# Retention followed by a SwiGLU layer on one core: the start as one list of single-engine steps, with the first pair of group 1 earlier and float32r products in five units

## The chip, the cores and the metric

The kernel runs on one core of a Trainium2 chip. The metric is the device time of one execution in microseconds (us), lower is better. A time is given as the median of three runs; the profile is of one execution of its own.

## What is computed

Four sequences of 768 tokens with 8 heads of 64 go through a retention layer (attention with a decay per head, kept as a running state from block to block). Its output, 3072 rows of 512, is normalised by its root mean square and goes through a gated layer with 1536 hidden units:

```python
for b in range(nb):
    intra = np.einsum('bhic,bhjc->bhij', qb, kb) * Dmask[None]
    intra = np.einsum('bhij,bhjd->bhid', intra, vb)
    inter = np.einsum('bhid,bhde->bhie', qb * lam_pow[None], kv_state)
    out[:, :, sl] = intra + inter
    kv_state = lam_block * kv_state + np.einsum('bhsd,bhse->bhde', kb_dec, vb)
rms = np.sqrt(np.mean(x * x, axis=-1, keepdims=True) + 1e-06)
xn = x / rms * rms_g
g = xn @ w_gate
silu = g * (1.0 / (1.0 + np.exp(-g)))
return (silu * (xn @ w_val) @ w_out).astype(np.float32)
```

## The kernel before

The rows are handled in six groups of 512 tokens. A group's retention is done in four pairs of heads (class `Pair`): `scores` (8 matmuls into `pa`, line 449), `decay_k` on ACT, `decay_a` on DVE (`a` from `pa` and the mask, L463), `decay_q` (L468), `state_sums` (`pst`, L477), `states` (L490, L492), `mix` (`po`, L504 and L512) and `keep`, which copies the output to `x` and squares it. `Norm` turns the squares into sums (`pss`, L565), a power on POOL (L576), and a spread over the partitions (`pr`, L582); then `high` (L624, L627) and `low` (L630) write x as an fp16 part `xh` and an fp16 rest `xl`.

The hidden layer is done in units of 128 hidden columns, 12 to a group (class `Hidden`). `gate` and `val` are 12 matmuls of 128x512 in fp16 each: in part 0 the high part of the weight by `xh`, in part 1 its low part by `xh`, in part 2 its high part by `xl`. `silu` is on ACT (L729), `mul` on DVE (L736), and `out` adds the unit's product with its rows of w_out into four accumulators. For `out` there are two forms: with `mul(True)` the hidden values stay float32 and each of the four matmuls is a float32 one against whole w_out rows (L659). Otherwise `high` (L746, ACT) and `low` (L753, DVE) split them into float32r parts, `split_o` (L238 on ACT, L239 on DVE) splits w_out likewise, and each tile is three float32r matmuls (L662 to L664).

Weights come as 64-bit numbers and are rebuilt on the chip (class `Weights`): `lift` on ACT (L214), `convert` on DVE (L223, L226), `square` on ACT (L382), a column-norm matmul (`pn`, L386), `scale` on DVE (L393, L397), then `high` on ACT (L404), `low` on DVE (L408), and `undo` (L414, L415). `lift_o` and `convert_o` do the same for w_out.

The order on all engines is written out by hand. Each call puts its instructions into the queues of its engines, which run them in that order. The order of the units is: group 0's units 0 to 5, all of group 1, group 0's units 6 to 11, then groups 2 to 5. `first_group` does group 0's four pairs, its norm and the first weights. `busy(n)` puts n float32 matmuls, which nobody reads, into PE's queue at the start (5 and 4) and around the norm (8 and 3). Then `first_unit`, `second_unit`, `scarce_unit` (three times) and `last_scarce_unit` do units 0 to 5 of group 0; all six use `mul(True)`. From unit 1 on each of the first four does one pair of group 1, and each converts the weights of the next unit. The units of group 1 do `split_o` for w_out's first six blocks. Loads are issued on SP, in an order that buffers decide: `load_next` takes the next one off a list.

Of the kernel before, what the change touches and what calls it, by code (L numbers as in the profile page):

```python
# [9 lines left out]
F32 = mybir.dt.float32  # L10
# [7 lines left out]
P = 128  # L18
# [5 lines left out]
def retention_swiglu_kernel(  # L24
# [67 lines left out]
    def load_gv(f):  # L92
        if f == 0:

            t = partial.bitcast(I32).rearrange("p a (b w) -> p (a b) w", w=2)
            t = t.rearrange("p (k o) w -> p k o w", k=2)
            for i in range(2):
                nc.sync.dma_start(t[:, i], w_all[f, :, i])
        else:
            t = stage.tile([P, 2, G, 2], I32, tag="in", name=f"raw_gv_{f}", bufs=4)  # L100
            nc.sync.dma_start(t, w_all[f, :, 0:2])
        raws[f] = t
# [10 lines left out]
    load_o(0)  # L113
    load_o(1)


    pending = []
    for i in range(NP):
        pending += [(load_gv, i + 1), (load_qkv, 1, i)]
# [35 lines left out]
    def powers(p):  # L155
        for h in (2 * p, 2 * p + 1):
# [4 lines left out]
        nc.vector.tensor_tensor_scan(  # L161
            pw[:, p, :], lam_p[:, p : p + 1].broadcast_to([P, P]), zeros, 1.0,
            ALU.mult, ALU.add,
        )
# [8 lines left out]
    def scales():  # L173
        gmax = const.tile([P, 1], F32, name="gmax")
# [3 lines left out]

        pmax = ps_out.tile([P, DM], F32, tag="po3", name="pmax")
        nc.tensor.matmul(pmax[:, :P], gmax.broadcast_to([P, P]), ident, start=True, stop=True)  # L180
        powers(0)
        nc.vector.tensor_reduce(gmax, pmax[:, :P], axis=mybir.AxisListType.X, op=ALU.max)
        ge = const.tile([P, 1], I32, name="ge")
        nc.vector.tensor_single_scalar(ge, gmax.bitcast(I32), 0x7F800000, op=ALU.bitwise_and)
        nc.vector.tensor_scalar_min(ge, ge, float(252 * EXP))
        sx = const.tile([P, 1], F32, name="sx")
# [49 lines left out]
    def split_o(f):  # L236
        wo[f] = t = wpool.tile([P, 2, DM], F32R, tag=f"wo{f}", name=f"wo_{f}")
        nc.scalar.copy(t[:, 0], whole_o(f))  # L238
        nc.vector.tensor_sub(t[:, 1], whole_o(f), t[:, 0].bitcast(F32))  # L239
# [103 lines left out]
    class Weights:  # L343


        def __init__(self, f, halves=False):
            self.f = f
            self.raw = raws.pop(f).rearrange("p k w o -> p (k w) o")
            if halves:

                ws = [op.tile([P, G], I32, tag="o", name=f"w_{f}_{i}") for i in range(2)]
            else:
                self.w = cvt.tile([P, 2 * G], I32, tag="w", name=f"w_{f}")
                ws = [self.w[:, i * G : (i + 1) * G] for i in range(2)]
            self.wi = ws
            self.ws = [w.bitcast(F32) for w in ws]
            self.ssq = small.tile([P, 2], F32, tag="ssq", name=f"ssq_{f}")
            self.bits = whole_o(f).bitcast(I32)

        def lift(self, i=None):  # L360
            if i is None:
# [14 lines left out]
        def convert_o(self):  # L376
            convert(self.bits, self.raw_o)
            load_o(self.f + 2)

        def square(self, i):  # L380
            junk = cvt.tile([P, G], mybir.dt.bfloat16, tag="junk", name=f"junk_{self.f}_{i}")
            nc.scalar.activation(junk, self.ws[i], AF.Square, accum_out=self.ssq[:, i : i + 1])  # L382

        def norm(self, pn, c=slice(0, 2)):
            self.pn = pn
# [20 lines left out]
        def low(self, i):  # L406
            hi, lo = ((wg, wv)[i][:, self.f, j] for j in range(2))
            nc.vector.scalar_tensor_tensor(  # L408
# [13 lines left out]
        def split(self):  # L422
            pn = ps_att.tile([P, 2, G], F32, tag="ps", name=f"pn_{self.f}")
            self.norm(pn[:, 0])
# [10 lines left out]
    class Pair:  # L435
# [3 lines left out]
        def __init__(self, m, p):  # L439
            self.m, self.p = m, p  # L440
            self.qT, self.kT, self.k, self.v = loaded.pop((m, p))
            self.odd = m == 0 and p % 2
# [11 lines left out]
        def decay_k(self):  # L454
            for j, r in enumerate(heads):
                last = mask[:, 2 * self.p + j, P - 1 : P]
# [8 lines left out]
        def decay_q(self):  # L465
            eng = nc.vector if self.m < 2 and (self.m, self.p) != (1, 0) else nc.gpsimd
# [30 lines left out]
        def mix(self):  # L497
            m, p = self.m, self.p
# [3 lines left out]
            for c in range(GC):  # L502
                for j, r in enumerate(heads):
# [3 lines left out]
                    )  # L507
            for c in range(GC):
# [8 lines left out]
        def keep(self):  # L517

            m, p = self.m, self.p
            if p == 0:  # L520
                x = xpool.tile([P, NK, G], F32, tag=f"x{SLOT_OF[m]}", name=f"x_{m}")
                if m:
                    sq = xpool.tile([P, GC, P], F32, tag="sq", name=f"sq_{m}")
                else:
                    sq = tmp.tile([P, GC, P], F32, tag="t", name=f"sq_{m}")
                rows[m] = x, [sq]
            x, sums = rows[m]
            sq = sums[0]
            s1 = sq
            if p:  # L530
                s1 = tmp.tile([P, GC, P], F32, tag="t", name=f"sq_{m}_{p}")
            if p < NP - 1:
                nc.scalar.copy(x[:, p, :].rearrange("p (c i) -> p c i", c=GC), self.po)
            nc.scalar.activation(s1, self.po, AF.Square)
            if p == NP - 1:
                nc.scalar.copy(x[:, p, :].rearrange("p (c i) -> p c i", c=GC), self.po)
            if m == 0 and p == NP - 1:
                sums.append(s1)
            elif p:
                last = m == 1 or p == NP - 1  # L540
                (nc.vector if last else nc.gpsimd).tensor_add(sq, sq, s1)
            load_next()

    class Norm:
# [11 lines left out]
        def sums(self, i=0):  # L556

            if i == 0:
                pss = ps_att.tile([P, 2, G], F32, tag="ps", name=f"pss_{self.m}")
                self.pss = pss[:, 0]  # L560
# [9 lines left out]

        def root(self):
            m = self.m
            ms = small.tile([P, GC], F32, tag="ms", name=f"ms_{m}")
            nc.vector.tensor_scalar(ms, self.pss4, 1.0 / DM, 1e-6, ALU.mult, ALU.add)
            self.y = small.tile([P, GC], F32, tag="y", name=f"y_{m}")
            nc.gpsimd.tensor_tensor(self.y, ms, power, op=ALU.pow)  # L576

        def spread(self):
            pr = ps_att.tile([P, 2, GC, P], F32, tag="ps", name=f"pr_{self.m}")[:, 0]
# [40 lines left out]
        def high(self, kk):  # L620
# [6 lines left out]
            nc.scalar.copy(self.xh[:, kk, :], xn)  # L627
# [4 lines left out]
        def parts(self):  # L632
            for kk in range(NK):
                self.high(kk)
# [64 lines left out]
    def finish(m, f, hh, hl, half):  # L699
        first = f == 0 or (m == 0 and f == HALF)  # L700
        last = f == NF - 1 or (m == 0 and f == HALF - 1)
        for t in range(GC):
            out_product(m, f, hh, hl, t, first, last, m == 0, half)

    class Hidden:


        def __init__(self, m, f):
            self.m, self.f = m, f
            self.half = m > 1  # L710
            self.x = xs[m]
# [5 lines left out]
        def gate(self, part=None, between=None):  # L717
            if not part:
                self.pg = ps_gv.tile([P, G], F32, tag="pg", name=f"pg_{self.m}_{self.f}")
            product(self.pg, *self.w[0], *self.x, part, between)  # L720

        def val(self, part=None, between=None):
            if not part:
                self.pv = ps_gv.tile([P, G], F32, tag="pv", name=f"pv_{self.m}_{self.f}")
            product(self.pv, *self.w[1], *self.x, part, between)
# [29 lines left out]
        def out(self):  # L755
            finish(self.m, self.f, self.hh, self.hl, self.half)
# [8 lines left out]
    def first_group():  # L765

        pair = [None] * NP
        busy(5)
        scales()
        busy(4)  # L770
        for p in range(NP):
            pair[p] = new = Pair(0, p)
            new.scores()
            new.decay_k()
            if p == NP - 1:
                wt = Weights(0)
                wt.lift()
            new.decay_a()
            if p < NP - 1:
                powers(p + 1)  # L780
            new.decay_q()
            if p:
                pair[p - 1].mix()
                pair[p - 1].keep()
            new.state_sums()
            new.states()
        new.mix()
        wt.convert(part=0)
        new.keep()
        nxt = Weights(1, True)  # L790
        nxt.lift(0)
        nxt.lift(1)
        norm = Norm(0)
        norm.sums(0)
        norm.sums(1)
        norm.root()
        wt.convert(part=1)
        wt.square(0)
        wt.square(1)
        busy(8)  # L800
        norm.spread()
        nxt.convert(0)
        nxt.square(0)
        pn = ps_out.tile([P, DM], F32, tag="po3", name="pn_0")
        wt.norm(pn)
        wt.scale()
        wt.high(0)
        norm.high(0)
        wt.high(1)
        norm.high(1)  # L810
        norm.high(2)
        norm.high(3)
        norm.low(2, nc.gpsimd)
        norm.low(3, nc.gpsimd)
        busy(3)
        nxt.norm(pn[:, 2:], slice(0, 1))
        wt.low(0)
        wt.low(1)
        wt.undo()
        nxt.scale(slice(0, 1))  # L820
        norm.low(0)
        norm.low(1)
        return wt, nxt

    def first_unit(h, wt_o, wt):

        h.gate(0)
        h.val(0)
        h.gate(1)
        h.val(1)  # L830
        wt.high(0)
        h.gate(2)
        h.val(2)
        wt.low(0)
        wt_o.lift_o()
        wt.convert(1)
        h.silu()
        wt.square(1)
        wt_o.convert_o()

    def second_unit(h, before, wt_o, wt, new):

        h.gate(0)
        wt_o.norm(ps_att.tile([P, 2, G], F32, tag="ps", name=f"pn_{wt_o.f}")[:, 0], slice(1, 2))
        h.gate(1)
        h.gate(2)
        wt_o.scale(slice(1, 2))
        wt_o.high(1)
        before.mul(True)
        wt_o.low(1)  # L850
# [253 lines left out]
```

## Time and profile before

| | |
|---|---|
| median of 3 runs | 685.96 us (685.9 to 686.19) |
| the profiled execution's own time | 685.8 us |
| its span, first to last instruction | 684.0 us |
| busy: PE, DVE, ACT, POOL | 673.3, 329.9, 246.2, 61.9 us |
| loaded and stored by DMA | 50.97 MB |

The span is the time between the first and the last instruction that the profiler saw; 1.8 us of the profiled execution lie around it. Busy times are sums over the whole span; PE is TensorE's matmuls, PEld its weight loads, which run beside them.

### The profile page before, as it was taken

Reading aid. Unit: us, or ns where it says so; the run is one execution under the profiler, and the core shown is the slowest. Engines: PE = TensorE matmul, PEld = TensorE weight load, DVE = VectorE, ACT = ScalarE, POOL = GpSimd, SP = SyncE. Lnnn points to the kernel's source line nnn. Section 1 sums busy time; section 2 is a strip of 40 time slices with the busy share of each in tenths; the row PEclk is TensorE's granted clock in tenths of the full one; section 3 lists DMA queues with packets and bytes.
Section 4 is the critical chain, followed back from the end, with each engine's and each line's share of the span. In section 5 each row is a group of like instructions: output and inputs, shape, how many; then the busy total and the mean of one; then the engine's idle time right before and its main releaser. Section 6 shows DMA issues by size and latency. Waiting matters only on the chain.

```text
span 684.0 us, 9838 instructions
## 1 busy us (share of the span) xinstructions
PE 673.3 (98%) x4118; PEld 359.5 (53%) x4118; DVE 329.9 (48%) x589; ACT 246.2 (36%) x434; POOL 61.9 (9%) x56
## 2 busy tenths in 40 slices
PE   8899999999999999999999999999999999999997
PEld 7645555556566555554444555444465444444443
DVE  6877677557557586644732322551332371221112
ACT  4656447545544523545222222231322231211111
POOL 0310000000002101434000111000012000000000
PEclk9999999999999999999999999999999999999999
DMA  8725652224213301223000131100100000100001
GB/s 322 294 93 171 278 197 93 92 93 154 63 62 124 124 1 40 73 75 114 10 1 1 62 123 63 62 1 1 61 2 1 0 1 1 61 1 1 0 1 61
DMA packets 14300, 50.97 MB, mean 75 GB/s; under 512 B 1712, under 2 KB 1968, under 8 KB 12848
## 3 DMA queue, kind: packets, MB, share of 16 engines
q1 hardware_dynamic: 13968, 49.69, 20.1%
q10 hardware_dynamic: 288, 0.66, 0.3%
q8 instruction: 32, 0.52, 0.3%
q14 instruction: 12, 0.10, 0.1%
HBM read 44.05 MB, written 6.29 MB: 74 GB/s over the span
## 4 chain that ended last, share of the span: by engine, by line
PE 96%; DVE 3%; POOL 0%; issue 0%; ACT 0%; DVEq 0%; POOLq 0%
PE pg L643 27%; PE pv L643 27%; PE acc L662 9%; PE acc L664 8%; PE acc L663 8%; PE pa L449 3%; PE acc L659 3%; PE po L504 3%; PE po L512 3%; PE pst L477 2%; DVE a L463 1%; PE unread L146 1%; PE pss L565 0%; DVE xn L624 0%; DVE state L492 0%; PE pr L582 0%
## 5 line engine op out<-in xcount | busy, mean ns | idle before, releaser
L643 PE MATMUL pg<-x,wg 128*128 128x512 f16 x864 | 199.9, 379 | 2.7 <-ACT x L627 1.6
L643 PE MATMUL pv<-x,wv 128*128 128x512 f16 x864 | 199.0, 379 | 0.0
L736 DVE SCALAR_TENSOR_TENSOR sg<-pv,cv,sg 128x512 f32<-128x512 f32 x48 | 36.0, 750 | 220.5 <-PE pv L643 220.5
L643 PEld LDWEIGHTS <-wg 128*128 128x128 f16 x864 | 82.6, 98 | 104.8 <-issue 9.2
L643 PEld LDWEIGHTS <-wv 128*128 128x128 f16 x864 | 84.5, 98 | 100.5 <-issue 0.4
L729 ACT ACTIVATE sg<-pg,cg 128x512 f32<-128x512 f32 x72 | 49.3, 685 | 150.6 <-PE pg L643 150.2
L664 PE MATMUL acc<-wo,hh 128*128 128x512 f16 (+1 forms) x264 | 101.2, 383 | 0.0
L663 PE MATMUL acc<-wo,hh 128*128 128x512 f16 (+1 forms) x264 | 101.1, 383 | 0.0
L746 ACT CAST hh<-sg 128x512 f16<-128x512 f32 (+1 forms) x66 | 40.8, 618 | 160.0 <-DVE sg L736 160.0
L662 PE MATMUL acc<-wo,hh 128*128 128x512 f16 x192 | 72.9, 380 | 0.0
L468 POOL TENSOR_TENSOR qkv<-qkv,pw 128x512 f32<-128x512 f32 x17 | 21.9, 1286 | 305.3 <-PE pa L449 305.3
L753 DVE TENSOR_TENSOR hh<-sg,hh 128x512 f16<-128x512 f32 x48 | 33.8, 703 | 24.6 <-ACT hh L746 24.6
L463 DVE TENSOR_TENSOR a<-pa,mask 128x1024 f32<-128x1024 f32 x24 | 29.4, 1224 | 8.0 <-PE pa L449 8.0
L662 PE MATMUL acc<-wo,hl 128*128 128x512 f32 x72 | 31.3, 435 | 0.0
L662 PEld LDWEIGHTS <-hh 128*128 128x128 f16 x192 | 18.8, 98 | 23.5 <-issue 2.4
L664 PEld LDWEIGHTS <-hh 128*128 128x128 f16 x192 | 18.8, 98 | 22.6
L663 PEld LDWEIGHTS <-hh 128*128 128x128 f16 x192 | 18.8, 98 | 20.8
L449 PE MATMUL pa<-qkv 64*128 64x128 f32 x384 | 27.9, 285 | 1.0 <-DVE a L463 1.0
L449 PEld LDWEIGHTS pa<-qkv 64*128 64x128 f32 x384 | 23.3, 187 | 10.1 <-issue 8.5
L504 PE MATMUL po<-a,qkv 128*64 128x128 f32 x384 | 25.7, 276 | 0.4 <-DVE a L463 0.4
L736 DVE SCALAR_TENSOR_TENSOR sg<-pv,cg,sg 128x512 f32<-128x512 f32 x18 | 13.5, 748 | 24.1 <-PE pv L643 24.1
L457 ACT ACTIVATE qkv<-qkv,mask 128x256 f32<-128x256 f32 x48 | 21.6, 500 | 5.3 <-DVE mask L157 3.3
(133 smaller groups left out, 629.4 us busy)
## 6 DMA issues: line engine op xcount, KB each, us to landing
qkv<-in_qkv_dram SPq DMA_DIRECT2D x47, 512.0 KB, 4.8
raw_gv<-in_weights_dram SPq DMA_DIRECT2D x11, 1024.0 KB, 7.6
raw_o<-in_weights_dram SPq DMA_DIRECT2D x12, 512.0 KB, 4.1
out_dram<-o SPq DMA_DIRECT2D x23, 256.0 KB, 2.5
partial<-in_weights_dram SPq DMA_DIRECT2D x2, 512.0 KB, 12.7
qkv<-in_qkv_dram ACTq DMA_DIRECT2D x1, 512.0 KB, 4.0
out_dram<-o SPq DMA_DIRECT2D x1, 128.0 KB, 2.1
out_dram<-o ACTq DMA_DIRECT2D x1, 128.0 KB, 2.0
```

What stands on the lines that cost most here:

```text
L449: nc.tensor.matmul(self.pa[:, j, c, :], self.kT[r, c, :], self.qT[r, c, :], start=True, stop=True,)
L463: nc.vector.tensor_mul(self.a, self.pa, decay.broadcast_to([P, 2, GC, P]))
L468: eng.tensor_mul(self.qT, self.qT, pw[:, p : p + 1, :].broadcast_to([P, GC, P]))
L504: nc.tensor.matmul(po[r, c, :], self.v[:, c, r], self.a[:, j, c, :], start=c == 0, stop=False, skip_group_check=True,)
L643: nc.tensor.matmul(ps, w[:, kk, :], x[:, kk, :], start=i == kk == 0, stop=i == 2 and kk == NK - 1,)
L662: nc.tensor.matmul(acc, hl[:, ts_], oh, start=first, stop=False)
L663: nc.tensor.matmul(acc, hh[:, ts_], ol, start=False, stop=False)
L664: nc.tensor.matmul(acc, hh[:, ts_], oh, start=False, stop=last)
L729: nc.scalar.activation(self.sg, self.pg, AF.Silu, scale=cg[:, self.f, 0:1])
L736: nc.vector.scalar_tensor_tensor(out, self.pv, factor, self.sg, ALU.mult, ALU.mult)
L746: nc.scalar.copy(self.hh, self.sg)
L753: nc.vector.tensor_sub(self.hl, self.sg, hh)
```

## The change

`first_group` and the six unit functions are replaced by one function, `ramp`, which calls single steps of pairs, norms, weights and units one after another. For that, methods are cut into parts that use one engine each (`mix` into `mix_chunks` and `mix_states`, `keep` into `keep_output`, `keep_squares` and `add_squares`, `high` of the norm into `scaled` and `high`, `split_o` into `high_o` and `low_o`, `powers` into three, `out` takes a list of tiles). What is done differently beyond the order:

- group 1's first pair (`p10`) has all its matmuls before the first gate matmul of group 0;
- units 0, 2, 3, 4 and 5 of group 0 use the float32r form of `out`, with their parts of w_out split in this stage; unit 1 stays float32;
- `out` is called tile by tile, between parts of other units' gate and val;
- the `busy` matmuls are kept in number (5, 4, 3, 8), with the first five after `pmax`;
- group 0's `decay_q` is on POOL, two of its `low` parts that were on POOL are on DVE, and the powers are all computed before the first `decay_a`;
- qkv of group 1's first pair is loaded before the weights of unit 1, and w_out's first blocks after those.

```diff
-    load_o(0)
-    load_o(1)
+    pending = [(load_qkv, 1, 0), (load_gv, 1)]
+    for i in range(1, NP):
...
-        if h.m == 1 and h.f < HALF:
+        if h.m == 1 and h.f < HALF and h.f not in wo:
             split_o(h.f)
...
+        largest()
+        pm = scales()
+        powers(0, 0)
...
+        p00.decay_k()
+        busy(5)
...
+        p00.scores()
+        busy(4)
+        p00.decay_a()
+        p00.decay_q(nc.gpsimd)
...
+        n0.sums(0)
+        n0.sums(1)
+        w0.square(0)
+        n0.mean()
+        w1.lift(0)
+        w1.lift(1)
+        p10.scores()
+        load_next()
+        p10.decay_a()
+        busy(3)
+        busy(8)
+        w1.convert(0)
+        w0.square(1)
+        w0.pn = w1.pn = ps_out.tile([P, DM], F32, tag="po3", name="pn_0")
+        w0.norm()
+        w1.convert(1)
...
+        p10.decay_q(nc.gpsimd)
+        p10.mix_states()
+        h0.gate(0)
+        h0.gate(1)
+        h0.val(0)
...
+        h0.out(3)
+        h0.out(0)
+        p10.keep_squares()
+        h2.val(1)
+        h0.out(1)
```

What this does to the queues shows at three places. PE, from the sums of group 0's squares to the first gate matmul. Before (`busy` is the tile `unread`, `pn` a column norm):

```order
L565 MATMUL pss_0_383<-ones_120,sq_0_3_372 128x128 x4
L146 MATMUL unread_401<-ident_115 128x128 x8
L582 MATMUL pr_0_410<-ident_115,y_0_394 128x128 x4
L386 MATMUL pn_0_419<-ssq_0_317,ones_120 128x2
L146 MATMUL unread_441<-ident_115 128x128 x3
L386 MATMUL pn_0_419<-ssq_1_380,ones_120 128x1
```

And now:

```order
L609 MATMUL pss_0_371<-ones_116,sq_0_3_363 128x128 x4
L475 MATMUL pa_1_0_389<-qkv_1_0_360 128x128 x8
L146 MATMUL unread_404<-ident_111 128x128 x3
L146 MATMUL unread_408<-ident_111 128x128 x8
L411 MATMUL pn_0_421<-ssq_0_380,ones_116 128x2
L631 MATMUL pr_0_436<-ident_111,y_0_434 128x128 x4
L411 MATMUL pn_0_421<-ssq_1_425,ones_116 128x1
L504 MATMUL pst_1_0_447<-qkv_1_0_360 64x64 x6
L535 MATMUL po_1_0_473<-a_1_0_402,qkv_1_0_360 64x128 x8
L411 MATMUL pn_1_492<-ssq_1_425,ones_116 128x1
L546 MATMUL po_1_0_473<-qkv_1_0_360,state_122 64x128 x6
```

The pair's four steps stand among the norm's, and all eleven `unread` matmuls stand ahead of the spread.

DVE, at the same place, now (from the mean of the squares to the last scaled x; before, nothing of pair 1_0 stood here and the second half of w_1 was converted later):

```order
L618 TENSOR_SCALAR ms_0_383<-pss_0_371 128x4
L491 TENSOR_TENSOR a_1_0_402<-pa_1_0_389,mask_123 128x1024
L230 TENSOR_SCALAR w_1_0_385<-w_1_0_385 128x512
L233 SCALAR_TENSOR_TENSOR w_1_0_385<-raw_gv_1_367,w_1_0_385 128x512
L230 TENSOR_SCALAR w_1_1_386<-w_1_1_386 128x512
L233 SCALAR_TENSOR_TENSOR w_1_1_386<-raw_gv_1_367,w_1_1_386 128x512
L418 TENSOR_SCALAR e2_0_430<-pn_0_421 128x2
L422 TENSOR_SCALAR sc_0_431<-e2_0_430 128x2
L673 SCALAR_TENSOR_TENSOR xn_0_0_444<-x_0_298,gs_125,pr_0_436 128x512
```

`decay_a` of the pair and both halves of w_1 stand ahead of the scaling that waits for the spread.

PE, in unit 2 of group 0, now (gate and val matmuls left out in the middle are those of one part; `acc` is an accumulator, its last number but one the tile):

```order
L714 MATMUL acc_0_0_3_652<-wo_0_597,hl_0_0_636 128x512
L715 MATMUL acc_0_0_3_652<-wo_0_597,hh_0_0_627 128x512
L716 MATMUL acc_0_0_3_652<-wo_0_597,hh_0_0_627 128x512
L714 MATMUL acc_0_0_0_656<-wo_0_597,hl_0_0_636 128x512
L715 MATMUL acc_0_0_0_656<-wo_0_597,hh_0_0_627 128x512
L716 MATMUL acc_0_0_0_656<-wo_0_597,hh_0_0_627 128x512
L695 MATMUL pv_0_2_622<-x_0_298,wv_131 128x512
```

Unit 0's product was four float32 matmuls in one block after unit 1's val; it is now three float32r matmuls a tile, in three blocks between parts of unit 2's gate and val.

## Rows read from the trace of the kernel before

**Rows 1.** Windows (start:end, length, busy us of PE, PEld, DVE, ACT, POOL, granted clock, DMA).
```profile
1.40:4.00 2.60, 2.54 (x11) 2.33 (x11) 0.33 (x2) 1.46 (x3) 0.10 (x3) 1.00 0.76 195
38.00:102.00 64.00, 64.00 (x420) 35.18 (x419) 45.24 (x89) 32.94 (x63) 2.39 (x2) 1.00 0.53 198
```
**Rows 2.** Chain that ended last, to 40 us (start, us, what).
```profile
6.35 1.12 PE pa L449 x16
...
7.49 1.22 DVE a L463
...
13.12 0.32 DVE pw L161
...
19.95 1.14 DVE a L463
...
23.04 2.00 PE pss L565 x16
...
27.34 1.16 PE pr L582 x8
...
29.02 2.62 DVE xn L624 x4
...
38.34 0.94 PE pg L643 x4
```
**Rows 3.** The same chain through unit 1 of group 0, a float32 product.
```profile
41.34 2.59 PE pv L643 x12
43.93 1.09 PE pa L449 x16
45.02 0.50 PE pst L477 x12
45.52 3.63 PE acc L659 x8
49.15 0.12 PE pn L386 x2
49.27 1.02 PE po L504 x16
50.29 0.80 PE po L512 x12
```
**Rows 4.** Timeline of PE in two units of group 1, float32r products.
```profile
118.02 2.75 PE L643 MATMUL pv<-x,wv 128*128 128x512 f16 x12
120.42 0.58 PE L662 MATMUL acc<-wo,hl 128*128 128x512 f32 x1
...
123.40 2.76 PE L643 MATMUL pg<-x,wg 128*128 128x512 f16 x12
```
**Rows 5.** Timeline from 24 to 34 us: PE's `busy`, and POOL beside DVE.
```profile
24.85 1.95 PE L146 MATMUL unread<-ident 128*128 128x128 f32 x16
...
32.05 2.83 POOL L630 TENSOR_TENSOR x<-xn,x 128x512 f16<-128x512 f32 x2 [4.76 <-ACT x L627]
32.22 1.64 DVE L408 SCALAR_TENSOR_TENSOR wv<-w,sc,wv 128x512 f16<-128x512 f32 x1
```
**Rows 6.** Groups of instructions, 0 to 110 us (busy us, mean ns, idle before).
```profile
L226 DVE SCALAR_TENSOR_TENSOR w<-raw_gv,w 128x1024 int32<-128x1024 int32 x5 | 6.1, 1226 | 0.2
L408 DVE SCALAR_TENSOR_TENSOR wg<-w,sc,wg 128x512 f16<-128x512 f32 x6 | 4.5, 748 | 3.2 <-ACT wg L404 3.2
L223 DVE TENSOR_SCALAR w<-w 128x1024 int32<-128x1024 int32 x6 | 4.1, 690 | 2.2 <-ACT w L214 2.2
L239 DVE TENSOR_TENSOR wo<-wg,wo 128x512 fp32r<-128x512 f32 x1 | 0.7, 683 | 0.0
```
**Rows 7.** DVE's waits, 36 to 103 us (waited for: us in total, times, longest).
```profile
DVE e L393 <- PE pn L386: 7.3, 5, 1.8
DVE wg L408 <- ACT wg L404: 3.2, 4, 0.8
DVE a L463 <- PE pa L449: 2.2, 4, 1.3
```

More of the change, by code (lines that the diff above doesn't have):

```diff
@@ L153, in retention_swiglu_kernel, with powers @@
     pw = const.tile([P, NP, P], F32, name="pw")
-    def powers(p):
-        for h in (2 * p, 2 * p + 1):
+    def powers(p, part):
+        if part < 2:
+            h = 2 * p + part
             nc.vector.tensor_tensor_scan(
@@ L440, in __init__ @@
             self.m, self.p = m, p
-            self.qT, self.kT, self.k, self.v = loaded.pop((m, p))
-            self.odd = m == 0 and p % 2
+            self.odd = m == 0 and p % 2 or m == 1 and p == 0
+        qT, kT, k, v = (property(lambda s, i=i: loaded[s.m, s.p][i]) for i in range(4))
         def scores(self):
@@ L452, in scores, with decay_k @@
                     )
-        def decay_k(self):
+        def decay_k(self, half=None):
             for j, r in enumerate(heads):
+                if half in (0, 1) and j != half:
+                    continue
                 last = mask[:, 2 * self.p + j, P - 1 : P]
@@ L517, in keep, with keep_output, keep_squares, add_squares @@
         def keep(self):
+            self.keep_output()
+            self.keep_squares()
+            if self.p:
+                self.add_squares(nc.vector if self.p == NP - 1 else nc.gpsimd)
+            load_next()
+        def keep_output(self, eng=nc.scalar):
             m, p = self.m, self.p
-            if p == 0:
+            if m not in rows:
                 x = xpool.tile([P, NK, G], F32, tag=f"x{SLOT_OF[m]}", name=f"x_{m}")
[L522 to L542, printed above, removed]
+                rows[m] = x, []
+            x = rows[m][0]
+            copy = nc.scalar.copy if eng is nc.scalar else eng.tensor_copy
+            copy(x[:, p, :].rearrange("p (c i) -> p c i", c=GC), self.po)
+        def keep_squares(self):
+            m, p = self.m, self.p
+            if m not in rows:
+                x = xpool.tile([P, NK, G], F32, tag=f"x{SLOT_OF[m]}", name=f"x_{m}")
+                rows[m] = x, []
+            if m and p == 0:
+                sq = xpool.tile([P, GC, P], F32, tag="sq", name=f"sq_{m}")
+            else:
+                sq = tmp.tile([P, GC, P], F32, tag="t", name=f"sq_{m}_{p}")
+            nc.scalar.activation(sq, self.po, AF.Square)
+            rows[m][1].append(sq)
+        def add_squares(self, eng):
+            sums = rows[self.m][1]
+            s1 = sums.pop(1)
+            eng.tensor_add(sums[0], sums[0], s1)
     class Norm:
@@ L618, in refine, with scaled @@
             )
-        def high(self, kk):
+        def scaled(self, kk):
             pool, tag = (hp, "hl") if self.m == 0 and kk > 1 else (tmp, "t")
@@ L633, in parts @@
             for kk in range(NK):
+                self.scaled(kk)
                 self.high(kk)
@@ L697, in out_product, with finish @@
         nc.sync.dma_start(rows_, o)
-    def finish(m, f, hh, hl, half):
+    def finish(m, f, hh, hl, half, ts=None):
         first = f == 0 or (m == 0 and f == HALF)
         last = f == NF - 1 or (m == 0 and f == HALF - 1)
-        for t in range(GC):
+        for t in ts or range(GC):
             out_product(m, f, hh, hl, t, first, last, m == 0, half)
@@ L719, in gate @@
                 self.pg = ps_gv.tile([P, G], F32, tag="pg", name=f"pg_{self.m}_{self.f}")
-            product(self.pg, *self.w[0], *self.x, part, between)
+            product(self.pg, *self.w[0], *xs[self.m], part, between)
         def val(self, part=None, between=None):
@@ L724, in val @@
                 self.pv = ps_gv.tile([P, G], F32, tag="pv", name=f"pv_{self.m}_{self.f}")
-            product(self.pv, *self.w[1], *self.x, part, between)
+            product(self.pv, *self.w[1], *xs[self.m], part, between)
         def silu(self):
@@ L763, in retention_swiglu_kernel @@
     SLOT_OF = {m: m % 2 if m < 2 else (m + 1) % 2 for m in range(NG)}
-    def first_group():
-        pair = [None] * NP
-        busy(5)
-        scales()
-        busy(4)
[L771 to L799, printed above, removed]
-        busy(8)
[L801 to L850, printed above, removed]
-        wt_o.undo()
-        wt.lift()
-        load_next()
-        h.silu()
-        new.decay_k()
-        h.val()
-        new.scores()
-        new.decay_q()
-        wt.convert()
-        wt.square(0)
-        wt.square(1)
-        new.decay_a()
-        new.state_sums()
-        new.states()
-        h.mul(True)
-        before.out()
-        finish_unit(wt_o, wt, new)
@@ L869, in scarce_unit @@
-    def scarce_unit(h, before, wt_o, wt, new):
-        h.gate()
-        wt.lift()
-        new.decay_k()
-        h.silu()
-        wt.convert()
-        h.val()
-        new.scores()
-        h.mul(True)
-        wt.square(0)
-        wt.square(1)
-        new.decay_a()
-        new.decay_q()
-        new.state_sums()
-        new.states()
-        before.out()
-        finish_unit(wt_o, wt, new)
-    def finish_unit(wt_o, wt, new):
-        wt.norm(ps_att.tile([P, 2, G], F32, tag="ps", name=f"pn_{wt.f}")[:, 0])
-        wt.scale()
-        wt.high(0)
-        wt.high(1)
-        new.mix()
-        wt.low(0)
-        wt.low(1)
-        wt.undo()
-        wt_o.lift_o()
-        wt_o.convert_o()
-        load_next()
-        new.keep()
```

495 lines of the change are left out of this document (397 added, 98 removed).

## The prediction

> **What bounds the kernel now.** I read the busy time by windows first, then the chain of work that ended last, then the timeline of the units, and last who waited for whom. By windows, PE is busy for all of 64 us from 38 to 102 us, at a granted clock of 1.00, with DVE at 45.24 [rows 1]. So in group 0's six units every microsecond of PE work that is removed comes off the end, as long as DVE keeps up; and from 102 us on, where group 1 begins, PE goes on as before and the change leaves its queue as it is. The chain shows the other stretch. Up to 38.34 us it goes back and forth between PE, DVE and POOL: first scores at 6.35, the four products with the mask from 7.49 to 19.95, sums of squares at 23.04, spread at 27.34, four scaled x at 29.02, and unit 1's gate at 38.34 [rows 2]. There PE is not the bound, the hand-overs are. The time after is therefore read as two sums: when unit 1's gate starts (38.34 now), and how much PE work is left from there to group 1.
>
> The sum is made against the profiled execution's own 685.8 us (span 684.0, and 1.8 around it). The median of the runs is 685.96, 0.16 above, which I add at the end.
>
> **Float32r in five units.** In unit 1 the float32 product takes 3.63 us on the chain [rows 3]. In group 1, val begins at 118.02 and the next gate at 123.40: 5.38, less val's 2.59, leaves 2.79 for the twelve float32r matmuls [rows 3, 4]. Each of the five units saves 0.84, in all **-4.2**. New work comes with it on engines that run beside PE: on DVE a rest of the hidden values and a rest of w_out a unit, 0.68 each by the row of w_out's, 6.8 in all [rows 6], and two casts a unit on ACT, which was busy 32.94 of the 64 [rows 1]. In group 1, DVE and ACT have the splits of five w_out blocks less; PE is the bound there, so that gains nothing.
>
> **Products tile by tile.** PE now enters a float32 or float32r stretch from fp16 about twelve times where it was seven, by the order. The rows bound what an entry costs: in [rows 4] val's twelve and the product's twelve fill their 5.38 us, and the 2.79 already hold one entry; by 12 times the mean step it would be nothing. The upper bound is the head start of 0.19 by which the first product's record begins before val's 2.59 are over [rows 3, 4]. Five entries cost 0 to 0.95. I take 0.05 each, **+0.25**, near the lower end, since the unit as a whole shows no gap.
>
> **The first pair of group 1.** It leaves the PE-bound stretch: scores 1.09, state sums 0.50, chunks 1.02, states' part 0.80, together 3.41 [rows 3]: **-3.4**. Its work goes ahead of the first gate, and what it costs there belongs to the next part. Its `decay_a` and state steps leave DVE's list in the units too.
>
> **The start, up to unit 1's gate.** The chain as it now runs, step by step.
> - PE's first matmul waits for `pmax`, that is for the constants (DVE's first work at about 3.7), no longer for the identity at 1.46. The first `busy` matmuls ran at half the later pace: eleven passes took 2.54 us, 0.23 each, where sixteen took 1.95, 0.12 each, at 24.85 [rows 1, 5], both with a granted clock of 1.00, the 2.4 GHz level. So `pmax` and five matmuls end at about 7.1, and the first scores at 8.2 if they run at full pace (1.12), at 9.3 if the slow pace lasts: 0.8 to 1.9 late. The powers cost nothing more: twelve scans of 0.33 [rows 2] end at 7.7.
> - The loop over the pairs gets shorter, since DVE no longer does scans and `decay_q` in it. From the first mask product to the last it took 12.46 [rows 2]; now PE's 3.41 a pair sets it, 10.2 in all. The last product starts at 18.5 to 19.6 instead of 19.95. But pair 2's `po` now stands between it and pair 3's, so pair 3's output ends 4.1 after that start, where it was 3.1. The sums start at 22.6 to 23.7, against 23.04. I take 23.0.
> - Then 2.00 for the sums, 1.09 for the pair's scores, 2.7 for eleven `busy` matmuls at 0.24, 0.12 for the norm: the spread starts at 28.9, 1.6 late; the power on POOL is done before that. The scaling of x starts 1.2 late, at 30.2, since the weight's scale stands ahead of it now. Four scalings (2.62) and three state steps (0.75) end at 33.6, a cast follows, and gate part 0 ends at 34.4. Five more parts of 0.86 give 38.75 for unit 1's gate, if the low parts come in time; two of those were on POOL and blocked the old gate part 2. Against 38.34: **+0.4**, with bounds of 0 and +1.1 from the bullets above.
>
> **POOL beside DVE.** In the old trace the fourth low part of a weight took 1.64 us where its kind takes 0.75 [rows 5, 6], and it started while POOL worked on two tiles of SBUF (32.05 to 34.88 [rows 5]). The price of a meeting is thus 0 to a whole POOL instruction, 1.42 (2.83 for two [rows 5]). Now pair 1_0's `decay_q` comes on POOL right behind the power, at about 27, where DVE converts both halves of w_1, which stand ahead of the scale and of x. I take somewhat under a third, **+0.4**: DVE has 1 us to spare there before the spread, and the spread is what it waits for. The Trainium skill says in "SBUF — State Buffer", section "SBUF: two separate sides", that the two engines share a port pair by an exclusive lock and the one that comes second blocks for the whole instruction. By that rule the cost would be the whole 1.42, and the time 1.0 above my forecast; the 1.64 agrees with it.
>
> **New waits in the units.** DVE's list there becomes 45.24, plus 6.8, plus 1.9 for unit 6's weights (0.69 and 1.23 [rows 6], which lay behind 102 us), less 2.0 for the pair: 52 us, in a stretch of about 57.8. That is 90%, where it was 71%. Following the queues by hand, the order always had the low part, the mask product or the rest ready before PE came to it, but by 0.1 to 0.4 us in several places. I take **+0.4**, with bounds of 0 and 3. DMA is no bound (0.53 busy [rows 1]); SP's queue holds unit loads behind w_out's, whose buffers free up when `convert_o` is done, some 10 us ahead of need.
>
> **Sum.** -4.2 - 3.4 + 0.25 + 0.4 + 0.4 + 0.4 = -6.15: 679.65, and with the 0.16, **679.8 us**.
>
> **The rivals.**
> - The pair finds no room. PE's idle time in the old start is made of short pieces, and all eleven `busy` matmuls are still there. If all of its 3.41 lengthen the start beyond what I have, the time is 683.2; if half, 681.5. For it: the spread alone is 1.6 late. Against it: the loop ahead is shorter, and the old gate's own waits fall away.
> - The start is late for its own reasons: the slow pace lasts through the first scores (+1.1 by the first bullet) and the POOL meeting costs all of 1.42 (+1.0). Together 681.9. The page "TensorE: Matmul & The Clock Gate", section "What's actually happening", of the Trainium skill says that the throttled state is the default and that activity releases it; by it a later first matmul means later full pace. The half pace at 1.46 agrees with that, the granted clock of 1.00 beside it does not.
> - Slower: DVE becomes the bound in the units. It works in order, and its three large waits of before, for the norms, for the casts of weights and for the scores, are 7.3, 3.2 and 2.2 us [rows 7]. If the new order fills none of them, DVE needs 52 + 12.7 = 64.7 for a stretch of 57.8: 6.9 more than forecast, 686.7. It decides from 11.9 us of kept waits on. For it: 90% is much for an engine that hands over to two others. Against it: the order places other work into exactly those waits, as conversions and rests.
> - The change does less than it says, because the float32r entries cost their upper bound: 0.7 more, 680.5, inside the range.
>
> **How the numbers follow.** The forecast with its bounds has a chance of 0.65, the pair without room 0.14, the late start 0.14, DVE as the bound 0.07. If nothing is lost in the start, in the units and at the POOL meeting, -8.2 is left, 677.8; the high end takes in half and most of the first rival and all of the second, 682.7. What a measurement can tell from no change is about 0.2%, 1.4 us: below 684.6 is faster, above 687.3 slower. All but the third rival and a tail of the first end below 684.6: faster 0.92. Of the DVE case half lies within: same 0.04, slower 0.04.
>
> **What would show it.** Group 1's first gate should start at about 96 us instead of 102.2, and unit 1's gate at 38.3 to 40. The acc groups of the first 100 us should show four float32 matmuls (eight passes) and sixty float32r ones. PE should be without waits over 0.3 us between these two points, DVE at about 90%. A start of unit 1's gate beyond 40.5 speaks for the first two rivals: long `L495` on POOL beside long DVE conversions at 26 to 28 us for the lock, scores of over 1.5 us at 7 to 9 us for the slow pace. PE waits of several us in total for DVE between 40 and 95 speak for the third. The forecast is wrong if group 1's gate starts after 99 us.

## The result, and the profile of the changed kernel

The changed kernel takes 678.85 us (median of 4 runs, 677.65 to 679.62) where the one before takes 686.08 (685.9 to 686.31): ratio 0.989, interval 0.9876 to 0.991. It is faster by 7.2 us. The forecast was 679.8. The profiled execution took 678.86 us, 6.94 less than the one profiled before, with a span of 677.1.

The chain of work that ended last, in order of time (start, length, what; a float32 matmul shows as two records, so five `busy` matmuls are x10), shows where unit 1's gate and group 1's first gate now start. To compare with [rows 2]:

```profile
3.58 0.17 DVE gmax L180
...
3.88 0.77 PE pmax L187 x2
4.65 2.13 PE unread L146 x10
6.78 2.01 PE pa L475 x16
8.79 1.47 PE unread L146 x8
...
22.86 1.98 PE pss L609 x16
24.85 1.09 PE pa L475 x16
25.94 0.88 PE unread L146 x6
...
29.06 1.14 PE pr L631 x8
...
30.23 1.40 DVE xn L673 x2
...
38.98 2.66 PE pg L695 x12
...
95.30 2.61 PE pg L695 x12
```

- Unit 1's gate starts at 38.98 instead of 38.34: the start is 0.64 us longer.
- Group 1's first gate starts at 95.30 instead of 102.30. The stage between the two went from 63.96 to 56.32 us, 7.64 less.
- 7.64 less and 0.64 more make 7.00. At the end of the execution 6.94 are left, so nothing of note changes from group 1 on.

In that stage PE works without a gap, as before [rows 1] (windows: busy us of PE, PEld, DVE, ACT, POOL, then the granted clock):

```profile
38.00:96.00 58.00, 58.00 (x389) 35.56 (x388) 47.30 (x92) 37.12 (x70) 2.17 (x2) 1.00 0.58 200
```

Since it never waits there, the chain of the stage is PE's work alone, and its shares by line say where the 7.6 us went. Before, over 63.96 us:

```profile
by line: PE acc L659 33.4%; PE pg L643 21.1%; PE pv L643 20.3%; PE pa L449 6.8%; PE po L504 6.4%; PE po L512 5.0%; PE pst L477 3.1%; PE pr L582 1.4%; PE pss L565 1.2%; PE pn L386 1.2%
```

After, over 56.32 us:

```profile
by line: PE pg L695 24.2%; PE pv L695 23.6%; PE acc L714 8.4%; PE acc L716 8.3%; PE acc L715 8.2%; PE acc L711 6.5%; PE pa L475 5.8%; PE po L535 4.7%; PE po L546 4.3%; PE pst L504 2.7%; PE pr L631 1.6%; PE pss L609 1.4%; PE pn L411 0.8%
```

With the durations of the chain's pieces added up by line, the products (`acc`) fall from 21.39 to 17.62 (-3.77). The pairs fall by 3.83, of which 3.41 is the pair that left (1.09, 0.50, 1.02 and 0.80) and 0.42 that the chunks (`po`, L504, now L535) of the other three take 0.88 instead of 1.02 each. The column norms fall from 0.80 to 0.48, since the second half of unit 1's, 0.32 on the old chain, now stands ahead of this stage. Gate and val rise by 0.22. Together that is -7.70, against 7.64 between the two starts.

Who waited for whom, PE from 1 to 98 us (total, times, longest):

```profile
PE pmax L187 <- DVE gmax L180: 3.9, 1, 3.9
PE pg L695 <- ACT x L678: 0.6, 2, 0.3
```

And DVE from 36 to 97 us, to compare with [rows 7]:

```profile
DVE xn L673 <- PE pr L631: 2.5, 1, 2.5
DVE hl L804 <- ACT hh L797: 1.8, 2, 1.1
DVE state L519 <- PE pst L504: 1.6, 2, 1.1
DVE sg L787 <- PE pv L695: 1.6, 3, 0.7
DVE e L418 <- PE pn L411: 1.4, 2, 0.8
```

PE waits for nothing in the units. DVE's waits for the column norms went from 7.3 to 1.4 us and those for the casts of weights and for the scores are not among them any more. Its new work fills part of them.

### The profile page after: what moved, and what is told of

It reads as the page before. It is cut to its first block, busy times and chain, and to the rows that moved or that the text cites. A ratio compares the mean times of both kernels' runs of the same rounds, so it can differ in the third digit from the quotient of the medians.

```text
span 677.1 us, 9894 instructions
## 1 busy us (share of the span) xinstructions
PE 668.6 (99%) x4138; PEld 362.6 (54%) x4138; DVE 328.9 (49%) x591; ACT 248.6 (37%) x439; POOL 64.1 (9%) x59
## 4 chain that ended last, share of the span: by engine, by line
PE 98%; DVE 1%; DMA 0%; ACT 0%; issue 0%; DVEq 0%
PE pg L695 28%; PE pv L695 28%; PE acc L714 10%; PE acc L716 9%; PE acc L715 9%; PE pa L475 4%; PE po L535 3%; PE po L546 3%; PE pst L504 2%; PE unread L146 1%; PE acc L711 1%; DMA cs<-in_consts_dram 0%; PE pss L609 0%; DVE xn L673 0%; PE pr L631 0%; PE pss L645 0%
## 5 line engine op out<-in xcount | busy, mean ns | idle before, releaser
L716 PE MATMUL acc<-wo,hh 128*128 128x512 f16 (+1 forms) x284 | 109.1, 384 | 0.0
L715 PE MATMUL acc<-wo,hh 128*128 128x512 f16 (+1 forms) x284 | 109.0, 384 | 0.0
L797 ACT CAST hh<-sg 128x512 f16<-128x512 f32 (+1 forms) x71 | 43.9, 618 | 166.1 <-DVE sg L787 166.1
L495 POOL TENSOR_TENSOR qkv<-qkv,pw 128x512 f32<-128x512 f32 x21 | 27.0, 1285 | 299.3 <-PE pa L475 299.3
L714 PE MATMUL acc<-wo,hl 128*128 128x512 f32 x92 | 40.6, 441 | 0.0
L787 DVE SCALAR_TENSOR_TENSOR sg<-pv,cg,sg 128x512 f32<-128x512 f32 x23 | 17.2, 748 | 27.3 <-PE pv L695 25.7
L535 PE MATMUL po<-a,qkv 128*64 128x128 f32 x384 | 25.3, 274 | 0.0
L566 ACT COPY x<-po 128x512 f32<-128x512 f32 x24 | 13.8, 582 | 29.4 <-PE po L546 29.3
```

What stands on the lines that cost most here:

```text
L495: eng.tensor_mul(self.qT, self.qT, pw[:, p : p + 1, :].broadcast_to([P, GC, P]))
L535: nc.tensor.matmul(po[r, c, :], self.v[:, c, r], self.a[:, j, c, :], start=c == 0, stop=False, skip_group_check=True,)
L714: nc.tensor.matmul(acc, hl[:, ts_], oh, start=first, stop=False)
L715: nc.tensor.matmul(acc, hh[:, ts_], ol, start=False, stop=False)
L716: nc.tensor.matmul(acc, hh[:, ts_], oh, start=False, stop=last)
L787: nc.vector.scalar_tensor_tensor(out, self.pv, factor, self.sg, ALU.mult, ALU.mult)
```

## The experiments

The theory after the result: the float32r products save some 4 us, the pair some 3.4, and the start gives back 0.6. The rivals: DVE as a limit in the units, a pair that has no room in the start, and a start that is late because of PE's slow pace. The experiments undo or isolate these, as far as one edit can. The timeline shows starts 0.1 to 0.2 us earlier than the chain, so starts are compared within one view.

### All six units with float32 products

The new order stays. w_out's first blocks are split in group 1 again.

```diff
-        h0.mul()
+        h0.mul(True)
...
-        high_o(0)
...
-        h0.high()
-        low_o(0, nc.vector)
...
-        h0.low()
```

The same is done for units 2 to 5.

> The changed kernel with all six units of group 0 in the float32 form; the splits of w_out's blocks go back to group 1. Theory (the product itself costs what PE takes): each of five products takes 3.63 us instead of 2.79, so +4.2 us, about 683.0, with unit 1's gate unchanged at 39.0 and group 1's first gate at about 99.5 instead of 95.3. Rival (DVE was the bound in the units, and the float32r work of 6.8 us on DVE and its casts on ACT cost time): the loss is clearly under 4.2, down to 2 or less.

Measured: 681.3 us (680.72 to 682.05), ratio 0.993 [0.9917, 0.9942]: 2.45 over the changed kernel, clearly under the 4.2 of the theory, which is the rival's sign. Where the rest went has to be read from the stage. PE's timeline at its two ends:

```profile
39.11 2.75 PE L695 MATMUL pg<-x,wg 128*128 128x512 f16 x12
...
98.33 2.75 PE L695 MATMUL pg<-x,wg 128*128 128x512 f16 x12
```

The stage takes 59.22 where the same view of the changed kernel gives 56.24 (38.90 to 95.14). Float32r is worth 3.0 us here, 0.6 a product, not 0.84. Added up along the chain, five float32r products take 13.97, 2.79 each as the prediction had it. But a float32 product in the new order takes 3.49 (six of them 20.94), where it took 3.57 on average before and 3.63 in the row that was read. What the prediction subtracted from was too large. PE waits as little as in the changed kernel (0.6 us in all for the casts of x, and for nothing in the units), so the rival's cause, waits for DVE, is not there.

### The pair back in unit 1

```diff
-        p10.scores()
         load_next()
-        p10.decay_a()
...
         h1.gate(1)
+        p10.scores()
+        p10.decay_q(nc.gpsimd)
+        p10.decay_a()
```

Its state and chunk steps go to unit 1 likewise.

> The changed kernel with the first pair of group 1 taken out of the start: its scores, mask product, states and output stand between unit 1's gate and val parts. Theory (the pair lay in the wait for the norms, and that wait is still there without it): group 1's first gate comes 2.0 to 3.4 us later (3.41 of PE work back in the units, less what the start gets shorter: its scores and state steps lie on the start's chain, 0 to 1.8), so 680.5 to 682.3. Rival (the pair found no room, and lengthened the start by what it saved): within 0.7 us of the changed kernel.

Measured: 681.8 us (681.33 to 682.93), ratio 0.9938 [0.9925, 0.9952]: 2.95 over the changed kernel. Group 1's first gate, in PE's timeline, and the first gate part of group 0:

```profile
31.66 3.76 PE L695 MATMUL pg<-x,wg 128*128 128x512 f16 x8 [1.78 <-ACT wg L429]
...
99.22 2.12 PE L695 MATMUL pg<-x,wg 128*128 128x512 f16 x9
```

By windows, the granted clock is the sixth figure after the length:

```profile
25.00:30.00 5.00, 4.57 (x36) 4.24 (x36) 3.06 (x8) 4.17 (x12) 1.06 (x1) 1.00 1.00 414
30.00:35.00 5.00, 2.94 (x8) 1.00 (x9) 4.97 (x10) 4.64 (x9) 1.16 (x1) 0.83 0.72 299
```

In the changed kernel 2.3 of the pair's 3.4 us of PE work lie where PE here waits 1.8 us for the weight's cast; the scores stand ahead of the spread. With the wait the granted clock falls to 0.83, between its two levels of 1.2 and 2.4 GHz: eight gate matmuls take 3.76 us, where eight of val take 1.89 in the changed kernel. The mean granted clock of the whole execution is 0.997 in all five runs, and 0.999 to 1.000 in the eight of the changed kernel.

So the room has two sides. Counted from the sums in PE's timeline, the pair makes the first gate matmul come 1.2 us later (9.94 instead of 8.75), but that gate then runs at full pace, and unit 1's gate comes 0.5 earlier than without the pair (16.11 instead of 16.59). What the pair would cost here at an unchanged clock was not tried.

### Without the eleven unread matmuls

```diff
-        busy(3)
-        busy(8)
```

> The changed kernel without the eleven unread matmuls between the pair's scores and the spread. Theory (PE is the bound there, DVE close behind): the norm's matmul can run at 27.1 instead of 28.75, but DVE has both halves of w_1 ahead of the scaling until 29.5, so the first scaled x starts at 29.9 instead of 30.2: -0.3 us, and at most -0.5. Rival 1 (the unread matmuls set the start): -1.5 to -2. Rival 2 (they keep PE's pace up, and without them matmuls of the norm and of the first gate run slower): +0.3 to +2, with gate matmuls of 0.43 us start to start instead of 0.22.

Measured: 679.86 us (679.22 to 680.44), ratio 0.9909 [0.9895, 0.9922]. Windows:

```profile
25.00:30.00 5.00, 2.57 (x27) 2.20 (x24) 4.18 (x8) 3.31 (x9) 2.20 (x2) 0.95 0.98 397
30.00:35.00 5.00, 5.00 (x45) 4.05 (x45) 4.84 (x12) 4.67 (x10) 1.16 (x1) 0.50 0.72 255
```

PE was busy for 2.57 of the 5 us before, and then ran at 0.50, the 1.2 GHz level, for all of the next five. Unit 1's gate starts at 40.65 instead of 38.90 in the timeline. The mean granted clock is 0.994 to 0.997 in all four runs. So the second rival held: the 2.9 us of unread work pay for themselves by 1 us, by the medians. That does not say that all eleven are needed; a run below leaves out three of them.

### The first unread matmuls ahead of the constants' maximum

```diff
+        busy(5)
         largest()
         pm = scales()
...
-        busy(5)
```

> The changed kernel with its first five unread matmuls ahead of the largest gain's matmul again, so that PE starts at 1.46 us instead of 3.88. Theory (the slow pace of PE's first microseconds ran into the first scores, 2.01 us instead of 1.12): the first scores start at 6.3 and take 1.1, the first mask product starts at 7.6, right behind the scans, instead of 8.84, and all behind it comes 1.0 to 1.3 us earlier: about 677.7, with less spread between runs than the 2 us of the changed kernel. Rival (the chain has room behind the first scores, or the loads set it): under 0.4 us earlier.

Measured: 678.9 us (677.11 to 678.99), ratio 0.9889 [0.9875, 0.9902], no gain. The theory fell: PE did have its first work at 1.46, but waited 1.95 us for the queries and keys, which landed at 6.30 (the loads of the rival), and the first scores were as slow as in the changed kernel. An early first matmul alone is not enough. Chain:

```profile
6.34 2.08 PE pa L475 x16
8.42 1.91 PE unread L146 x8
```

### The whole start of before: unread, maximum, unread, scores

```diff
+        busy(5)
         largest()
         pm = scales()
+        busy(4)
...
-        busy(5)
...
         p00.scores()
-        busy(4)
```

> The changed kernel with the start's unread matmuls as they were before the change: five, the largest gain's matmul, four, and then the first scores. With the five alone ahead, PE stood still for 2.0 us in front of the first scores and they took 2.08 us again. Theory (the pace of the first scores hangs on PE working without a gap up to them): they take 1.12 us from about 6.35, the first mask product starts at 7.6 instead of 8.84, the sums at about 21.9 instead of 22.86 and group 1's first gate at about 94.4 instead of 95.3: -0.9 us, about 678.0. Rival (the chain is set behind the first pair by the landing of unit 0's weights at 18.8 us and by ACT's work on them): the sums start at most 0.3 us earlier and the time stays within 0.4 us.

Measured: 677.38 us (676.86 to 677.61), ratio 0.9872 [0.9859, 0.9886]. Chain:

```profile
1.47 2.50 PE unread L146 x10
3.97 0.57 PE pmax L187 x2
4.54 1.71 PE unread L146 x8
6.24 1.57 PE pa L475 x16
```

PE is without a gap from 1.47 us on, the scores come 0.5 us sooner and take 0.4 less, and nothing unread stands behind them. Unit 1's gate starts at 37.55 and group 1's first at 93.90 in the timeline. Run once more beside the last two kernels below:

> The same kernel as the one with the start of before, once more, beside the next two: within 0.7 us of 677.4 by the theory that its start saves the time; if the unchanged kernel's 678.1 was the same number with luck in it, 678 to 679.

Measured: 677.42 us (677.06 to 677.71), ratio 0.9873 [0.9858, 0.9887]. It repeats; there the first scores took 1.16.

### Float32r in the old order

```diff
-        h.mul(True)
+        h.mul()
+        h.high()
...
+        h.low()
...
+        if before.f != 1:
+            split_o(before.f)
```

This is the kernel before, with five of its six units in the float32r form.

> The kernel before the change, with its order and its six unit functions, but with float32r parts of w_out in units 0, 2, 3, 4 and 5, each split in the next unit and the splits taken out of group 1. Theory (PE is the bound in the units, and a float32r product is 0.6 us shorter in PE's queue, as the all-float32 run showed): -3.0 us or nearly, about 683.1. Rival (the new order is what makes room for the float32r work on DVE and ACT, in the old order PE waits for it): PE waits for hl, wo or x in every unit, the time stays within 1 us of 686.1 or goes above it.

Measured: 683.95 us (683.67 to 684.34), ratio 0.997 [0.9958, 0.9981]: 2.0 less than before, between the theory (3.0) and the rival (at most 1). PE's timeline:

```profile
38.59 1.02 PE L643 MATMUL pg<-x,wg 128*128 128x512 f16 x4
...
99.09 0.82 PE L643 MATMUL pg<-x,wg 128*128 128x512 f16 x3
100.79 1.46 PE L643 MATMUL pg<-x,wg 128*128 128x512 f16 x6 [0.88 <-ACT x L627]
```

The stage takes 60.50, where the same view of the kernel before gives 63.88 (38.25 to 102.13): 3.38 less. Of that, 0.34 is lost ahead of it, in an execution whose granted clock was 0.71 from 30 to 35 us (1.00 in the kernel before, which has the same waits there), and 0.88 goes to a new wait in group 1's first gate: the cast of x for the next norm is not ready when PE gets there sooner. So the old order can't use all of it, the new one can. Against this kernel the one with the pair put back has the same work in the stage, in 59.72 (39.50 to 99.22): the order alone takes 0.78 out of it, of which 0.42 is the chunks, and the pair 3.48. The three steps, 3.38, 0.78 and 3.48, make up the whole 7.64.

### Eight unread matmuls, and the second half of w_1 later

From the start of before, `busy(3)` is taken out, and w_1's second half is converted and normed beside group 0's first gate:

```diff
-        busy(3)
...
-        w1.convert(1)
...
+        w1.convert(1)
         p10.decay_q(nc.gpsimd)
...
+        w1.norm(slice(1, 2))
         h0.val(2)
```

> The run with the start's unread matmuls as before the change, and also with eight of the eleven unread matmuls ahead of the spread, and with the second half of unit 1's weights converted behind the scaled x instead of ahead of it. Theory (between the pair's scores and the spread PE's unread matmuls are the bound, and DVE's conversions stand 0.4 us behind them): the spread starts 0.75 us earlier against the sums, and DVE is free for it: 0.6 to 0.8 us faster than with the start alone changed. Rival 1 (PE's pace falls when unread matmuls are taken out, as in the run without them): a granted clock under 1.00 between 30 and 40 us, and 0.5 to 1.5 us slower than it. Rival 2 (the later conversion is late for unit 0's val and unit 1's): waits of PE of over 0.3 us between 36 and 42 us.

Measured: 678.78 us (678.69 to 678.83), ratio 0.9894 [0.9879, 0.9909], 1.4 more than with the start of before alone, and 1.7 more than the kernel further below that also has the eight matmuls but not the move. The granted clock stays at 1.00 from 20 to 40 us, so the first rival fell; the second held. Timeline:

```profile
37.75 0.38 PE L411 MATMUL pn<-ssq,ones 128*128 128x1 f32 x2 [1.72 <-ACT junk L407]
```

What was gained ahead of the gate is paid by a wait for the squares inside it.

### The changed kernel, once more

> The changed kernel itself once more, on the chip of this call: 678.9 within 0.5 us, with the 2 us of spread between its runs.

Measured: 678.1 us (677.54 to 678.79), ratio 0.9884 [0.9871, 0.9898]. In its profiled execution (677.54) the chain reads:

```profile
6.81 1.22 PE pa L475 x16
8.03 1.09 PE unread L146 x8
```

The same instructions took 2.01 and 1.47 in the first profile, 1.17 us more, and the two executions differ by 1.32. From these two places on they run alike to within 0.2 us. In this execution unit 1's gate starts at 37.84 on the chain, 1.14 earlier than in the first profile and 0.50 earlier than before the change. With both sets, the change has eight runs around 678.6 (677.54 to 679.62), the start of before eight around 677.4 (676.86 to 677.71). The quickest runs of the one reach the other's, so what the start of before saves fits the slow first scores that it avoids; which of the unprofiled runs had them is not on record.

### Eight unread matmuls alone, and the norm between the gate's parts

The first has only `busy(3)` taken out of the kernel with the start of before:

> As the control beside it, with eight unread matmuls instead of eleven ahead of the spread's sums. Theory (the unread matmuls are work on the path, each 0.14 us): spread 0.4 us sooner, and 0 to 0.3 us less in all, since VectorE stands next there. Rival (the three keep the granted clock up): a granted clock below 0.9 between 30 and 40 us and 0.5 to 1 us more.

Measured: 677.06 us (676.86 to 677.85), ratio 0.9867 [0.985, 0.9883]. By the intervals it can't be told from its control. The granted clock stays at 1.00 from 20 to 40 us, so the rival fell: eight unread matmuls do as well there as eleven.

The second also moves `w1.norm` between parts of unit 1's gate. For that it puts the conversion of w_1's second half behind the scaled x, and moves the norm of its first half and the pair's state steps too, so it does not isolate the one move:

> As the kernel with eight unread matmuls, and the second half of w_1 is converted and its norm put inside unit 1's gate, after the gate's first part. Theory (the norm's matmul and its wait for ScalarE then lie beside work of the gate): 0.6 to 0.9 us less than the control. Rival (TensorE waits again, for the squares or for VectorE's later turn): no gain, or up to 1.4 us more, as with the later conversion alone.

Measured: 678.96 us (678.45 to 680.3), ratio 0.9898 [0.9884, 0.9913]. It is 1.9 over its control: the theory fell as with the later conversion, and the rival held. Timeline of PE:

```profile
38.69 1.02 PE L695 MATMUL pg<-x,wg 128*128 128x512 f16 x4 [1.83 <-ACT sg L780]
```

And of ACT:

```profile
36.79 0.63 ACT L407 ACTIVATE junk<-w 128x512 bf16<-128x512 f32 x1 [2.11 <-DVE w L233]
...
37.97 0.66 ACT L780 ACTIVATE sg<-pg,cg 128x512 f32<-128x512 f32 x1
```

The squares wait 2.11 us on ACT for DVE's conversion, and unit 0's silu is queued behind them; unit 1's gate needs the accumulator that silu reads.

## Why the prediction was right, point by point

The time lies 0.95 below the forecast and inside its range. Against the profiled execution -6.94 stands beside -6.15. The mechanism was right: the two savings come off a stretch in which PE never waits. The terms around them were not all right, and that they nearly cancel is in part luck.

- **Float32r and its entries** (-4.2 and +0.25, together -3.95): -3.77. A float32r product takes the 2.79 that was read. The float32 product was mis-sized: 3.63 is what each of the first four takes, but the last two stand back to back and take 6.87 together, so that the mean of the six is 3.57. In the chain of the kernel before:

```profile
95.43 6.87 PE acc L659 x16
```

This is the one saving that was put too high, by 0.4 before the entries, and nearly all of that is these two. The stage as a whole gives 3.38 for float32r in the old order and 2.98 in the new one. An entry's price was not measured apart; as the 2.79 holds for products in three blocks too, the lower end is what the chain bears out.
- **The pair** (-3.4): right, 3.41 on the chain and 3.48 between two kernels of equal work. That it is free in the start hangs on the granted clock, which the prediction did not reckon with.
- **New waits in the units** (+0.4, bounds 0 and 3): none. DVE is busy for 47.30 of 58.00, 82%, where 90% was forecast; the conversion of unit 6's weights, 1.9 of the forecast's 52, still stands behind group 1's first gate (97.07 in DVE's timeline). DVE as the bound, the rival on the slower side, has nothing for it. (By the forecast's own 52 and 57.8, DVE would have begun to bind at 5.8 us of kept waits; 11.9 is where the stage would be no shorter than before.)
- **What the sum left out**: chunks and column norms get 0.74 shorter by the order (0.32 of it moved ahead of the stage), and gate and val 0.22 longer. With the waits that did not come, this is why the stage gave 7.64 where 6.95 was forecast.
- **The start** (+0.4) **and the POOL meeting** (+0.4): +0.64 together, all of it the start's. The sums start at 22.86 (forecast 23.0), the spread at 29.06 (28.9), the scaling at 30.23 (30.2). The slow pace did reach the first scores (2.01 us), which was half of the second rival, and the shorter loop over the pairs paid for it, as the step on the loop had it. In the second profile of the same kernel it did not reach them, and unit 1's gate came 0.50 earlier than before the change, outside the bounds of 0 and +1.1. So how near the start's sum came is luck.
- **The low end of the range** does not follow from the terms. Without the losses in the start, in the units and at the meeting -4.2 - 3.4 + 0.25 = -7.35 is left, not -8.2, and the time 678.6, not 677.8. The measured 678.85 lies above both.
- **The meeting itself** shows in the timeline of POOL:

```profile
26.19 1.28 POOL L495 TENSOR_TENSOR qkv<-qkv,pw 128x512 f32<-128x512 f32 x1
```

and of DVE:

```profile
25.98 1.23 DVE L491 TENSOR_TENSOR a<-pa,mask 128x1024 f32<-128x1024 f32 x1 [0.94 <-PE pa L475]
27.12 0.63 DVE L230 TENSOR_SCALAR w<-w 128x512 int32<-128x512 int32 x1
...
28.40 0.42 DVE L230 TENSOR_SCALAR w<-w 128x512 int32<-128x512 int32 x1
...
30.23 1.40 DVE L673 SCALAR_TENSOR_TENSOR xn<-x,gs,pr 128x512 f32<-128x512 f32 x2 [0.41 <-PE pr L631]
```

The conversion that begins 0.35 us before POOL ends takes 0.21 more than its twin. In the kernel with the pair put back, where POOL does nothing at that time, the same conversion takes 0.43. The product with the mask, which reads one operand from PSUM, takes no longer than elsewhere. The 0.21 costs the kernel nothing: DVE still waits 0.41 us for the spread afterwards. So the term of +0.4 was too large by all of itself, not a little.

The trace of before has a second meeting, beside the 1.64 that the prediction read:

```profile
33.78 1.12 DVE L414 TENSOR_SCALAR inv<-e 128x2 int32<-128x2 int32 x1
```

This takes 0.16 elsewhere, and POOL's two tiles end at 34.88 [rows 5]. It loses 0.96 where 1.10 of POOL's work is left, the conversion 0.21 of 0.35. So in both cases the delay is what is left of POOL's instruction, less 0.14. The 1.64 is 0.89 over its kind too, not the whole 1.42. By the Trainium skill ("SBUF — State Buffer", section "SBUF: two separate sides") the engine that starts first keeps the shared ports for its whole instruction and the other blocks. These delays agree with that, but for the 0.14, if what is left of the instruction is counted, and not with the whole instruction that the prediction took from it.

- **The pair without room** fell by the kernel that puts it back: 2.95 slower.

## What to carry to other kernels

A stage in which the bound engine never waits can be forecast from its own instructions, by their durations in the place that they come from; take the mean of all instances, not one row. Work moved out of such a stage can cost little where that engine waits anyway. Here, without the pair or without the unread matmuls in that place, PE waited and the granted clock fell, so work that fills a wait ahead of a hand-over can earn its time; how much of it is needed has to be tried, as eight of the eleven matmuls did as well. Where a kernel starts, check that its first real work follows filler without a long gap.

## What was not expected of the hardware

PE's pace in the first microseconds is not what the granted clock's column says: it reads 1.00 throughout. Where PE's first matmul came at 3.9 us or later, or came at 1.46 and a wait of 1.95 us stood ahead of the scores, the first sixteen passes of scores took 2.01 to 2.08 in five profiled executions and 1.22 in one. Where PE worked from 1.46 us on with at most 0.7 us of waiting ahead of the scores, they took 1.1 to 1.6 in all seven. The Trainium skill ("TensorE: Matmul & The Clock Gate", section "What's actually happening") says that the throttled state is the default and that activity releases it; the dependence on early work with little waiting agrees, the column does not. Why one of the six was quick stays open: its kernel is the same as that of one of the slow ones.

The chunks of a pair (L535) take 0.88 us right behind state sums and 1.02 behind the states' part, as the chain of the changed kernel shows for two pairs of group 0:

```profile
18.75 0.61 PE pst L504 x16
19.36 0.88 PE po L535 x16
20.23 0.80 PE po L546 x12
21.04 1.02 PE po L535 x16
```

Which property of the work ahead does that was not tried.
